# The last two blocks of the last expert become a third pair whose first layer is seven products of halves

## The chip, the cores and the metric

One core of one Trainium2 chip. The time is that of one run of the whole program, in microseconds (us) of device time; lower is better. The program is shown through one profiled execution, whose own time is given beside the median of the timed runs. TensorE is called PE, VectorE DVE, ScalarE ACT, GpSimd POOL and SyncE SP, as in the profile.

## The reference

```python
# attention with decay, then a mixture of 4 experts over 2304 tokens, then 8 slot experts
scores = scale * q @ k.T + decay;  attn = softmax(scores, causal);  x = attn @ v     # x: 2304 x 512
p = domain_probs / domain_probs.sum(-1)
for e in range(4):
    h = np.maximum(x @ w1[e], 0.0)            # w1[e]: 512 x 1024
    out += p[:, e:e + 1] * (h @ w2[e])        # w2[e]: 1024 x 512
logits = out @ phi                            # 32 slots
d = softmax(logits, axis=0);  slot_input = d.T @ out
slot_out[e2] = relu(slot_input[e2] @ w1_2[e2]) @ w2_2[e2]     # 8 experts, 4 slots each
result = softmax(logits, axis=1) @ slot_out
```

## The kernel before, in words

The change lies in the first mixture of experts, in its last expert (e = 3). The 2304 tokens are 18 tiles of 128; three tiles are a block of 384 tokens, and blocks 0 to 5 cover all. Every float32 factor is held as a high and a low half-precision part, and each product is three matmuls (high by high, high by low, low by high).

A block's expert is two layers. The plain first layer (mm_l1, L642) is 8 groups of 12 matmuls, each 128x128 by 128x384 into one PSUM bank; of each group ACT makes the high part of relu (L648) and DVE the low part (L651). The plain second layer (mm_l2, L660) makes 24 matmuls of 128x512 for one tile, and DVE adds the result, weighted, to the tile's sum (L666).

Where two blocks are a pair, the first layer is cheaper. x of the two blocks and w1 are cut into halves, and seven products of halves (each 6 matmuls of 128x384, with sums of halves of x named s1 to s4 made once and kept) give what eight would. One `quad` (L872 to L900) does this for one of four pieces of 128 columns of the first layer's two halves. Its products come in the order m1, m2, m5, m6, m7, m4, m3, in three kinds of PSUM bank, qA, qF and qE. Between them ACT copies a bank into SBUF (L895) and takes relu (L883), and DVE adds a copy into a bank or into SBUF (L879, among these the add called t22 below) and makes low parts (L886). Some products wait for these: m7 accumulates into the qA bank that ACT has to have copied after m6 (the copy c6), and m4 into the qA bank of which t22 was made after m7. A second form, `quad_sums`, also halves the second layer; its products of the second layer are L1081.

Before the change expert 3 has two pairs (blocks 0 to 3), both in the second form, and blocks 4 and 5 are done plainly: for each, 8 groups of L642 and then three tiles of L660.

After expert 3 has finished a block, its "post" work goes on beside the next block: transposes pt (L2325, copied by ACT L2329 and DVE L2327), logits lg (L2335, with a maximum on DVE and exponentials on ACT), a transpose dt (L2353), slot sums sl (L2360), a transpose ct (L2376, with DVE L2379, L2380, ACT L2382, DVE L2383), and then the split of the result (DVE L2388, and L2390 three times) and one DMA that transposes it (L2392), which is issued from ACT's queue. The last block's post is done tile by tile (L2317 for its pt, copied by ACT L2320). In between stand the two small transposes sel (L2238), written into the first bank of a PSUM pool that is opened when the q banks are given up. Then come the slot experts (L2580, L2597), whose 33.5 MB of weights are loaded by SP (`fill`, L2272) as pages of SBUF come free.

Each engine takes its instructions in the order in which the program issues them. For DVE, ACT, POOL and SP that order comes from a planner with a cost for every task (the number in `T("DVE", 0.55, ...)`); PE's order inside a pair is written out (`in_order`), with `beside()` where one piece of post work is slipped in. Behind the pairs all is in the order of the code.

Of the kernel before, what the change touches and what calls it, by code (L numbers as in the profile page):

```python
# [9 lines left out]
F32 = mybir.dt.float32  # L10
# [3 lines left out]
AF = mybir.ActivationFunctionType  # L14
# [10 lines left out]
T_W, CAP_W = 15, 60  # L25
X_SHIFT = 4
C_MUL = 1024.0
PAIRS = (0, 3, 3, 2)
PLAIN = (0, 1, 0, 0)
ORDER = ((), (0, 1, 2), (2, 0, 1), (0, 1))  # L30
OUT_H = ((), (1, 2), (0, 1), (0, 1))
T_SO = 13
BIG = float(2 ** 23)
# [261 lines left out]
def moe_attention_kernel(ctx: ExitStack, tc: tile.TileContext, q, k, v, f, probs, w1, w2, phi, s1, s2, out):  # L295
# [354 lines left out]
    def ev_l1_b(ps, m):  # L650
        nc.vector.scalar_tensor_tensor(out=hl[:, m], in0=ps, scalar=0.0, in1=hh[:, m], op0=ALU.max, op1=ALU.subtract)  # L651

    def mm_l2(e, j, t, ms=range(KF), ps=None):
        if ps is None:
            ps = ps_m.tile([128, DM], F32, tag="m", name="pso")
        ts = slice(t * 128, (t + 1) * 128)
        h_, l_ = hT2[j % 2 if j < 2 * PAIRS[e] else 0]
# [157 lines left out]
    def halves_tasks(e, w1_t, w2_t, s_t, tmps, between=lambda j: [], used_up=None, plain_t=None, next_x=None, t_sums=None):  # L815
# [39 lines left out]
        def quad(p, m, h_t):  # L855
# [23 lines left out]
                return T("DVE", 0.55, -30, lambda: nc.vector.tensor_tensor(out=out(), in0=x(), in1=y(), op=ALU.add), deps)  # L879

            def split(i, c, y, t, give=None):
                h_, l_ = (z[:, y] for z in hT2[i])
                t = T("Act", 0.52, -30, lambda: nc.scalar.activation(out=h_, in_=c(), func=AF.Relu), [t])  # L883

                def lo():
                    nc.vector.scalar_tensor_tensor(out=l_, in0=c(), scalar=0.0, in1=h_, op0=ALU.max, op1=ALU.subtract)  # L886
                    if give:
                        later(lambda: q_used.update({give: q_used[give] - 1}))
                h_t[i][y] = t = T("DVE", 0.62, -30, lo, [t])
                return t  # L890
# [283 lines left out]
        for p in ORDER[e]:  # L1174
# [801 lines left out]
    with tc.manual_schedule():  # L1976
# [117 lines left out]
        def sums_of_x(p, key, tmp, deps):  # L2094
            s_t[p] = steps(key, x_sums(p, lambda: [page(x, 2)[:, 0:2 * NB] for x in tmp]), X_COST, deps)
# [6 lines left out]
        s_d = [[dram.tile([128, 2 * NB], F32, name=f"sd{p}{i}") for i in range(4)] for p in range(NBLK // 2 - 1)]  # L2102

        def s_place(p, i):
            n = len(p_S[p])
# [19 lines left out]

        def keep_s(p):
            return [T("DMA", 1.0, 90, lambda i=i: nc.sync.dma_start(out=s_d[p][i], in_=s_place(p, i)), s_t[p]) for i in range(4)]
        kept_s = {1: keep_s(1)}
        HOME = 0
        for k, p in (((1, 1), 1), ((1, 2), 2), ((2, 2), 2), (None, HOME)):  # L2130
            xR[k] = [xT[2 * p], xT[2 * p + 1], xS[p]]
# [17 lines left out]
        hq_own[1, 2] = {"11": h_of(xT_page[0]), "22": h_of(xT_page[1])}  # L2149
        hq_own[1, 1] = {**hq_own[1, 2], "12": h_of(wA + 4)}  # L2150
        hq_free[1, 1] = {"11": kept_x[0], "22": kept_x[1], "12": s_t[2]}
        hq_free[2, 0] = {"11": kept_x[4], "22": kept_x[5]}
        hq_free[1, 2] = {"12": kept_x[3], "4": kept_x[2]}
        end_s1, end_1, _ = halves_tasks(1, w1_1 + e0_t, w2_1 + pw_t, s_t, tmps, plain_t=(w1_p, e0_t, plain_l1),
# [19 lines left out]
        def next_2(p, t, old):  # L2174
            i = ORDER[2].index(p) + 1
            n = (ORDER[2] + ORDER[3])[i]
            if n in s_t:
                (x_2 if i < 3 else x_3)[n] = load_x(n, [t])
            else:
                back = [T("DMA", 2.0, 30 + x, lambda x=x: nc.sync.dma_start(out=page(xT_page[x], 3), in_=x_d[x]),  # L2180
                          kept_x[x] + [prod[1, 2, i, t] for i in (1, 4) for t in range(TPB)] + raw_end[x]) for x in range(2)]
                sums_of_x(n, 59.8, (n_kn, n_kn + 3), back + [t] + old)
# [23 lines left out]
        kept = {acc_page[T] for T in range(NTILE)} | set(range(hT_p, hT_p + 6)) | set(range(raw2, raw2 + 6)) | {wA + 14, wA + 15} | set(range(p0_, p0_ + 6))  # L2206
# [198 lines left out]
        def used_up(p):  # L2405
            if p == 0:
                dyn.free(p0_, 6)
            if p == PAIRS[e] - 1:
                dyn.free(raw2, 6)
            fill(0)  # L2410

        def next_3(p, t, old):
            x_3[p + 1] = load_x(p + 1, [t], p + 1 < PAIRS[e])
            if p + 1 == PAIRS[e]:
                b12, am = page(wA + 14, 2).rearrange("p (k n) -> p k n", k=2), ams["w1", e]
                y = T("DMA", 1.46, 29, lambda: nc.sync.dma_start(
                    out=b12, in_=w1[e, 0:256, 512:1024].rearrange("(k p) n -> p k n", p=128)), w1_3)
                y = T("Act", 1.14, 62, lambda: nc.scalar.activation(out=wS[e][3][:, 0], in_=b12, func=AF.Copy,
                                                                    scale=am[:, 7:8]), [y, t])
                end_b.append(T("DVE", 1.28, 62, lambda: nc.vector.scalar_tensor_tensor(  # L2420
                    out=wS[e][3][:, 1], in0=b12, scalar=am[:, 7:8], in1=wS[e][3][:, 0], op0=ALU.mult, op1=ALU.subtract),
                    [y], sb=2))
        end_b = []
        end_s3, end_3, rest = halves_tasks(e, [], [], x_3, tmps, between, used_up, next_x=next_3, t_sums=sums_3)
        end_3 = end_3 + end_b
# [4 lines left out]
        for p in t_pages + p_T + [wA + 14]:  # L2430
            dyn.free(p, 2)
        for p in h_pages:
            dyn.free(p, 3)
        for x in range(2):
            xT_page[NBLK - 2 + x], xT[NBLK - 2 + x] = xT_page[x], xT[x]
# [12 lines left out]
        j = NBLK - 1  # L2448
        for mm, ev in moe_quanta(e, j)[:KF]:
            ev(mm())  # L2450
            step(1 + (len(side) > KF))
        while side:
            step(1)
        dyn.free(xT_page[j], 3)
        for p in w_pg:
            dyn.free(p, 2)
        fill(0)
        cells = {}
# [8 lines left out]
        def part(t, ms):  # L2467
            cells[t] = mm_l2(e, j, t, ms, cells.get(t))
            if ms[-1] == KF - 1:
                ev_l2(cells[t], e, j, t)  # L2470

        def second_w(i):

            for p in p_w[0]:
                dyn.free(p + i)
            fill(0)
        po = [post([j * TPB + t], j) for t in range(TPB)]
        (tr0, lg0, dt0, sl0), (tr1, lg1, dt1, sl1), (tr2, lg2, dt2, sl2) = (x[0] for x in po)
# [7 lines left out]
        part(2, (0, 1))  # L2486
        second_w(0)
        rest.pop()()
        tr1()
        sl0()  # L2490
        part(2, (2,))
        rest.append(lg1())
        part(2, (3,))
        second_w(1)
        part(2, (4, 5))
        second_w(2)
        dt1()
# [212 lines left out]
```

## Time and profile before

| | |
|---|---|
| timed runs | 965.05 us median of 3 (964.74 to 966.63) |
| profiled execution, its own time | 965.62 us |
| its span, first to last instruction | 963.9 us |
| mean granted TensorE clock | 0.995 |
| busy PE, DVE, ACT, POOL | 925.5, 696.8, 501.6, 447.8 us |

The span is shorter than the execution's own time by 1.7 us, which lie around the instructions. An engine's busy share is a mean over stages with different limits; a stage's own limit is read from its windows and waits. Ends of matmuls are modelled, so two following matmuls overlap by a little in the rows; the step from one start to the next is the measured one.

### The profile page before, as it was taken

What the parts mean: (1) busy time and instruction counts of PE and PEld (TensorE: products, weight loads), DVE (VectorE), ACT (ScalarE), POOL (GpSimd) and SP (SyncE); (2) the same over time, 40 slices, a digit from 0 to 9 for tenths busy, and PEclk for the clock granted to TensorE, in tenths of its full rate; (3) what the DMA queues carried; (4) which work ended last, traced back from release to release, by engine and by line L of the source; (5) the groups of instructions that cost most, each with busy time, mean ns of one, the idle gap of its engine ahead of it and who ended that gap; (6) DMA issues with size and microseconds to landing.
All of it is one profiled execution on the core that took longest, in us unless ns stands there. A gap on an engine that the chain in (4) does not pass through costs nothing.

```text
span 963.9 us, 22484 instructions
## 1 busy us (share of the span) xinstructions
PE 925.5 (96%) x9092; PEld 637.4 (66%) x9092; DVE 696.8 (72%) x1329; ACT 501.6 (52%) x1115; POOL 447.8 (46%) x440
## 2 busy tenths in 40 slices
PE   6988999999999999999999999999999999999994
PEld 3567778788778775456868645686868768655331
DVE  6989987878786579959779796868976585433313
ACT  5887888877787565446053842525453250212123
POOL 3998786786664368435058323635543150000000
PEclk9999999999999999999999999999999999999998
DMA  8889999999999740341202444231413032954695
GB/s 225 190 158 176 187 189 187 184 205 166 203 163 246 127 165 35 137 142 60 89 1 67 153 153 153 95 114 44 169 65 132 1 97 82 382 175 134 192 361 196
DMA packets 265320, 144.51 MB, mean 150 GB/s; under 512 B 230880, under 2 KB 230880, under 8 KB 265216
## 3 DMA queue, kind: packets, MB, share of 16 engines
q1 hardware_dynamic: 263088, 142.51, 58.2%
q8 instruction: 71, 1.16, 0.5%
q10 hardware_dynamic: 2128, 0.57, 0.3%
q14 instruction: 33, 0.27, 0.1%
HBM read 88.78 MB, written 12.58 MB: 105 GB/s over the span
## 4 chain that ended last, share of the span: by engine, by line
PE 75%; DVE 13%; issue 3%; ACT 2%; POOL 2%; DMA 2%; SPq 1%; DVEq 0%; ACTq 0%; POOLq 0%
PE qA L942 9%; PE qA L1081 7%; PE pso L1144 6%; PE psh L599 6%; PE pso L620 6%; PE qE L942 5%; PE qE L1081 5%; PE psh L642 3%; PE qF L1081 3%; PE pso L660 3%; PE s L1579 3%; PE pso L1081 2%; PE qF L942 2%; PE pv L1668 2%; DVE arena L552 2%
## 5 line engine op out<-in xcount | busy, mean ns | idle before, releaser
L1081 PEld LDWEIGHTS <-arena 128*128 128x128 f16 x1512 | 147.8, 98 | 21.1 <-issue 1.8
L942 PEld LDWEIGHTS <-arena 128*128 128x128 f16 x1008 | 98.4, 98 | 66.5 <-issue 3.8
L1448 POOL TENSOR_SCALAR arena<-arena 128x384 f16<-128x384 f32 (+5 forms) x77 | 56.8, 741 | 136.2 <-ACT arena L953 76.1
L972 POOL TENSOR_TENSOR arena<-arena 128x384 f16<-128x384 f32 x78 | 78.6, 1017 | 75.0 <-ACT arena L1446 73.4
L942 PE MATMUL qA<-arena 128*128 128x384 f16 x576 | 104.5, 326 | 0.7 <-DVE arena L959 0.3
L599 PE MATMUL psh<-arena 128*128 128x128 f16 x1728 | 101.9, 219 | 0.0
L620 PE MATMUL pso<-arena 128*128 128x512 f16 x432 | 100.6, 384 | 0.0
L599 PEld LDWEIGHTS <-arena 128*128 128x128 f16 x1728 | 97.4, 98 | 0.4
L1446 ACT ACTIVATE arena<-arena 128x384 f16<-128x384 f32 (+5 forms) x137 | 79.6, 593 | 29.7 <-DVE arena L964 22.2
L1620 ACT ACTIVATE arena<-s,mx,qs 128x320 f32<-128x320 f32 (+4 forms) x144 | 91.5, 641 | 4.8 <-POOL arena L1637 1.8
L1637 POOL TENSOR_TENSOR arena<-arena 128x128 f16<-128x128 f32 (+4 forms) x79 | 69.5, 901 | 12.9 <-ACT arena L1446 11.1
L704 POOL TENSOR_TENSOR arena<-arena 128x768 f32<-128x768 f32 (+2 forms) x23 | 46.4, 2024 | 54.8 <-DVE arena L704 37.6
L1600 DVE TENSOR_REDUCE mx<-s 128x1 f32<-128x576 f32 (+4 forms) x76 | 64.3, 848 | 8.1 <-PE s L1579 7.8
L620 PEld LDWEIGHTS <-arena 128*128 128x128 f16 x432 | 40.5, 99 | 44.4 <-issue 2.1
L1579 PE MATMUL s<-arena 128*128 128x128 f16 (+1 forms) x928 | 65.1, 212 | 4.3 <-ACT arena L1620 3.4
L1081 PE MATMUL qA<-arena 128*128 128x256 f16 x576 | 68.8, 273 | 0.0
L1144 PE MATMUL pso<-arena 128*128 128x512 f16 x288 | 63.3, 379 | 0.0
L1579 PEld LDWEIGHTS <-arena 128*128 128x128 f16 x928 | 57.5, 98 | 7.1 <-issue 5.2
L552 DVE SCALAR_TENSOR_TENSOR arena<-arena,wm 128x512 f16<-128x512 f32 x44 | 55.3, 1269 | 1.9 <-ACT arena L549 1.9
L1637 DVE TENSOR_TENSOR arena<-arena 128x64 f16<-128x64 f32 (+4 forms) x69 | 49.9, 760 | 6.6 <-POOL arena L1448 3.4
L942 PE MATMUL qE<-arena 128*128 128x384 f16 x288 | 53.7, 326 | 0.1
L953 ACT ACTIVATE arena<-qA 128x384 f32<-128x384 f32 x48 | 23.3, 486 | 57.9 <-PE qA L942 56.8
(277 smaller groups left out, 1872.8 us busy)
## 6 DMA issues: line engine op xcount, KB each, us to landing
arena<-in_moe_w_dram SPq DMA_DIRECT2D x61, 512.0 KB, 4.6
arena<-in_moe_w_dram SPq DMA_DIRECT2D x63, 256.0 KB, 5.1
arena<-xd SPq DMA_DIRECT2D x10, 768.0 KB, 4.3
arena<-in_moe_w_dram SPq DMA_DIRECT2D x7, 1024.0 KB, 9.0
arena<-in_moe_w_dram SPq DMA_DIRECT2D x7, 768.0 KB, 10.6
xd<-arena SPq DMA_DIRECT2D x6, 768.0 KB, 7.1
arena<-sd SPq DMA_DIRECT2D x12, 384.0 KB, 6.1
arena<-in_k_dram SPq DMA_DIRECT2D x16, 256.0 KB, 3.7
```

The source lines that it names most:

```text
L552: return lambda: nc.vector.scalar_tensor_tensor(out=wS[e][o][:, 1, c], in0=b, scalar=am[:, 7:8], in1=wS[e][o][:, 0, c], op0=ALU.mult, op1= ...
L599: nc.tensor.matmul(out=ps[:, m, :], lhsT=wt["w1" + a, 0][:, kk, ms], rhs=xT[j][:, b + kk, ts], start=(n == 0), stop=(n == 3 * KD - 1))
L620: nc.tensor.matmul(out=ops[u], lhsT=a[:, m, ts], rhs=wt["w2" + b, 0][:, m, :], start=(m == 0 and z == 0), stop=(m == KF - 1 and z == 2))
L942: nc.tensor.matmul(out=ps[c], lhsT=wS[e][o][:, w, k, ms], rhs=a[z][:, k], start=(first and i == 0), stop=(i == 5), skip_group_check=True)
L972: h_t[q][m] = y = T(LO, {"DVE": 0.55, "Pool": 1.0}, -30, lambda eng: by[eng].tensor_tensor(out=l_, in0=a, in1=h_, op=ALU.subtract), [y], r ...
L1081: nc.tensor.matmul(out=ps[c, t], lhsT=hq[a][x][:, m, ts], rhs=wq[y][:, m, :], start=(first and m == 0 and n == 0), stop=(m == KF // 2 - 1 ...
L1144: nc.tensor.matmul(out=cell[0], lhsT=a[:, m, ts], rhs=wt["w2" + b, e][:, m, :], start=(len(left) == KF - 1 and z == 0), stop=(not left and ...
L1446: nc.scalar.activation(out=out, in_=x, func=AF.Copy, scale=scale)
L1579: nc.tensor.matmul(out=o, lhsT=qT[u][:, 2 * h + w, :], rhs=kT[kk][:, 2 * h + w, k0:k0 + n_], start=(w == 0), stop=(w == 1 and mask is None))
L1600: nc.vector.tensor_reduce(out=mx[:, 0:nh].rearrange("p (a h) -> p a h", a=sv.shape[1]), in_=sv, axis=AX.X, op=ALU.max, negate=True)
L1620: nc.scalar.activation(out=P[:, x], in_=sv[:, x // hb, x % hb], func=AF.Exp, scale=qs[u][:, 4:5], bias=mxs[n][:, 4 + x:5 + x], accum_out=s ...
L1637: by[eng].tensor_tensor(out=t[:, :, d0:d0 + n_], in0=P[:, :, s0:s0 + n_], in1=t[:, :, s0:s0 + n_], op=ALU.subtract)
```

## The change

Expert 3 gets a third pair, blocks 4 and 5. Its first layer is four `quad`s; then follow the plain second layers of both blocks, block 4's three tiles and block 5's three tiles (`part`). The sums s1 to s4 of these blocks, which were made before expert 1, are saved to DRAM (`keep_s(2)`) and loaded again; this replaces one 512 KB load of a quarter of w1 and the ACT and DVE instruction that split it again (L2416 to L2420). The post of block 2 is slipped between the products of the third pair, that of block 3 between second layers of block 4, and that of block 4 between second layers of block 5. SBUF pages come free in another order.

```diff
-PAIRS = (0, 3, 3, 2)
+PAIRS = (0, 3, 3, 3)
-ORDER = ((), (0, 1, 2), (2, 0, 1), (0, 1))
+ORDER = ((), (0, 1, 2), (2, 0, 1), (0, 1, 2))
...
+    def h_at(e, i):
+        return 1 - i if e == E - 1 else i
...
             def split(i, c, y, t, give=None):
-                h_, l_ = (z[:, y] for z in hT2[i])
+                h_, l_ = (z[:, y] for z in hT2[h_at(e, i)])
...
                 if before:
                     beside()
                 next(g)
+                if e == E - 1:
+                    if m == 1:
+                        in_order(0.0, lambda: used_up(-1), [], lambda: True)
+                    if before:
+                        beside()
                 before = g
+            if e == E - 1:
+                next(before)
+                beside()
+                next(before, None)
+                end_s.append(last[-1])
+                in_order(0.0, lambda p=p: used_up(p), [], lambda: True)
+                end.extend(y for z in h_t for y in z.values())
+                continue
...
-        kept_s = {1: keep_s(1)}
+        kept_s = {1: keep_s(1), 2: keep_s(2)}
...
-        for j in range(2 * PAIRS[e], NBLK - 1):
-            for x, (mm, ev) in enumerate(moe_quanta(e, j)):
-                ev(mm())
-                if x == KF - 1:
-                    dyn.free(xT_page[j], 3)
-                    side.append(fill)
-                step(1 + (len(side) > 11 - x))
-            a, z = post(list(range(j * TPB, (j + 1) * TPB)), j)
-            side += a + z + [fill]
+        cells = {}
+
+        def part(k, ms):
+            j, t = NBLK - 2 + k // TPB, k % TPB
+            cells[k] = mm_l2(e, j, t, ms, cells.get(k))
+            if ms[-1] == KF - 1:
+                ev_l2(cells[k], e, j, t)
...
+        for ms in ((0, 1), (2, 4), (5, 6), (3, 7)):
+            part(0, ms)
+            step(2)
+        for ms in ((0, 1), (2, 3)):
+            part(1, ms)
+            step(2)
+        part(1, (4, 5))
+        step(2)
+        part(1, (6, 7))
...
+        part(2, range(KF))
...
+        a, z = post(list(range((j - 1) * TPB, j * TPB)), j - 1)
+        a = [x for x in a if x] + z
+        for k, ms, n in ((3, (0, 1), 1), (3, (2, 3), 1), (3, (4, 5), 1), (3, (6, 7), 1), (4, (0, 1), 2), (4, (2, 3), 2)):
+            part(k, ms)
+            for _ in range(n):
+                a.pop(0)()
...
-        part(0, range(8))
-        part(1, range(4))
         tr0()
-        part(1, (4, 5))
+        part(4, (4, 5))
         rest = [lg0()]
-        part(1, (6, 7))
+        part(4, (6, 7))
         dt0()
```

Three places where the order of an engine is another. Line numbers of the changed kernel are a few higher: L875 is the matmul of a product, L882 the add, L886 relu, L889 the low part, L898 the copy, L663 the second layer's matmul, L2396 to L2400 the DVE and ACT work behind ct, L2405 and L2407 the split, L2409 the DMA that transposes, L2255 and L2256 sel, L2337 the copy of a tile's pt.

ACT, where the second quad of the third pair begins (qA_11567, qF_11574 and qE_11582 are the banks of the first quad, qA_11632, qF_11641 and qE_11650 those of the second; DMA_TRANSPOSE belongs to the post of block 1). In the change:

```order
L898 ACTIVATE arena_64<-qA_11632 128x384
L886 ACTIVATE arena_64<-qF_11641 128x384
L898 ACTIVATE arena_64<-qE_11650 128x384
L2409 DMA_TRANSPOSE arena_64<-arena_64 128x3x128
L886 ACTIVATE arena_64<-qA_11567 128x384
L898 ACTIVATE arena_64<-qA_11632 128x384
L886 ACTIVATE arena_64<-qE_11582 128x384
```

The same DMA_TRANSPOSE in the kernel before, among the relus of the plain first layer of block 4:

```order
L648 ACTIVATE arena_64<-psh_11608 128x384
L648 ACTIVATE arena_64<-psh_11629 128x384
L2392 DMA_TRANSPOSE arena_64<-arena_64 128x3x128
L648 ACTIVATE arena_64<-psh_11649 128x384
L2329 ACTIVATE arena_64<-pt_11664 128x384
```

Where a relu of the plain first layer stood behind the transposing DMA, there now stand a relu of the first quad and then the second quad's copy c6 (the second row with qA_11632), for which its m7 waits.

DVE at the end of the third pair, in the change (qA_11720 and qE_11737 are banks of the third quad, qA_11812 and qE_11829 of the fourth; ct_11875 is that of the post of block 2):

```order
L882 TENSOR_TENSOR qE_11737<-qE_11737,arena_64 128x384
L889 SCALAR_TENSOR_TENSOR arena_64<-qE_11737,arena_64 128x384
L2396 TENSOR_REDUCE arena_64<-ct_11875 128x3
L2397 TENSOR_TENSOR arena_64<-ct_11875,arena_64 128x96
L2400 TENSOR_REDUCE arena_64<-arena_64 128x3
L882 TENSOR_TENSOR arena_64<-qA_11812,arena_64 128x384
L889 SCALAR_TENSOR_TENSOR arena_64<-arena_64 128x384
L2405 TENSOR_SCALAR arena_64<-arena_64 128x6x32
L2407 SCALAR_TENSOR_TENSOR arena_64<-arena_64 128x2x32 x3
L889 SCALAR_TENSOR_TENSOR arena_64<-qA_11812,arena_64 128x384
L882 TENSOR_TENSOR qE_11829<-qE_11829,arena_64 128x384
L889 SCALAR_TENSOR_TENSOR arena_64<-qE_11829,arena_64 128x384
```

The sixth row is t22 of the fourth quad, now behind three rows of the post of block 2, and the last row, the last use of a q bank, is behind that post's split. On PE m7 of the fourth quad, ct, m4 and m3 follow each other here, then six matmuls L663 and sel.

ACT where the post of block 4 ends, in the change; the DMA_TRANSPOSE is that of block 4, and L2337 is the copy of pt of tile 15, the first tile of block 5:

```order
L2360 ACTIVATE arena_64<-lg_12111,arena_64 96x128
L2363 ACTIVATE arena_64<-arena_64 96x1
L2399 ACTIVATE arena_64<-arena_64 128x96
L2409 DMA_TRANSPOSE arena_64<-arena_64 128x3x128
L2337 ACTIVATE arena_64<-pt_12173 128x4x128
L2360 ACTIVATE arena_64<-lg_12185,arena_64 32x128
```

ACT's order is the same here before and after, but on PE 36 + 6 matmuls L660 stood between this ct and the logits of tile 15 (the pt of that tile among them), and now six do.

## Rows read from the trace of the kernel before

**Rows 1.** The page: busy time of the engines; the chain that ended last.
```profile
PE 925.5 (96%) x9092; PEld 637.4 (66%) x9092; DVE 696.8 (72%) x1329; ACT 501.6 (52%) x1115; POOL 447.8 (46%) x440
...
PE 75%; DVE 13%; issue 3%; ACT 2%; POOL 2%; DMA 2%; SPq 1%; DVEq 0%; ACTq 0%; POOLq 0%
```

**Rows 2.** Windows: length, then busy us and count of PE, PEld, DVE, ACT, POOL.
```profile
785.00:800.00 15.00, 15.00 (x127) 12.13 (x125) 13.66 (x32) 5.52 (x11) 5.53 (x6) 1.00 0.77 268
819.00:900.00 81.00, 81.00 (x521) 44.75 (x519) 31.39 (x94) 15.19 (x43) 0.00 (x0) 1.00 0.66 228
930.00:940.00 10.00, 10.00 (x89) 3.12 (x85) 0.29 (x1) 2.39 (x4) 0.00 (x0) 1.00 0.84 322
948.00:950.00 2.00, 0.38 (x4) 0.14 (x2) 1.51 (x2) 1.55 (x3) 0.00 (x0) 1.00 0.01 3
```

**Rows 3.** Timeline of PE, plain layers, and all L642 (ns min/median/max): start, us, line.
```profile
823.60 4.06 PE L642 MATMUL psh<-arena 128*128 128x384 f16 x24
827.50 1.47 PE L2325 MATMUL pt<-ident,arena 128*128 128x128 f32 x12
...
879.57 7.93 PE L660 MATMUL pso<-arena 128*128 128x512 f16 x36
887.34 0.60 PE L2317 MATMUL pt<-ident,arena 128*128 128x128 f32 x4
887.78 1.46 PE L660 MATMUL pso<-arena 128*128 128x512 f16 x6
...
L642 PE MATMUL psh<-arena x192: 323/326/337, 821.4 to 878.2; 128*128 128x384 f16 x192
```

**Rows 4.** Timeline of PE, end of expert 2's quads; L872's idle over all four.
```profile
558.11 1.14 PE L872 MATMUL qA<-arena 128*128 128x384 f16 x6
559.08 2.75 PE L1144 MATMUL pso<-arena 128*128 128x512 f16 x12
561.67 1.14 PE L872 MATMUL qA<-arena 128*128 128x384 f16 x6
...
  issue: 0.3, 1
```

**Rows 5.** ACT and DVE work of expert 2's quads, by line: ns min/median/max.
```profile
L879 DVE TENSOR_TENSOR arena<-qA,arena x4: 544/546/557, 538.6 to 560.9; 128x384 f32<-128x384 f32 x4
L883 ACT ACTIVATE arena<-qA x4: 490/490/491, 542.3 to 562.8; 128x384 f16<-128x384 f32 x4
L886 DVE SCALAR_TENSOR_TENSOR arena<-qF,arena x4: 545/552/557, 535.3 to 555.9; 128x384 f16<-128x384 f32 x4
L895 ACT ACTIVATE arena<-qA x8: 471/486/491, 532.7 to 557.6; 128x384 f32<-128x384 f32 x8
```

**Rows 6.** The DMA issued from ACT, L2392, and ACT around the one at 842.06.
```profile
L2392 ACTq DMA_TRANSPOSE arena<-arena x5: 1197/1359/1804, 797.7 to 882.2; - x5
...
842.06 1.20 ACTq L2392 DMA_TRANSPOSE arena<-arena  x1
843.31 0.49 ACT L648 ACTIVATE arena<-psh 128x384 f16<-128x384 f32 x1 [2.35 <-issue]
```

**Rows 7.** Timelines of PE, DVE and ACT: posts of blocks 0 and 4, from ct on.
```profile
793.35 0.25 PE L2376 MATMUL ct<-ident,arena 96*128 96x96 f32 x1
793.43 1.47 PE L1081 MATMUL pso<-arena 128*128 128x256 f16 x12
...
793.63 0.26 DVE L2379 TENSOR_REDUCE arena<-ct 128x3 f32<-128x96 f32 x1
...
794.70 0.47 DVE L1092 SCALAR_TENSOR_TENSOR arena<-qA,pw,arena 128x256 f32<-128x256 f32 x1
...
880.27 0.25 DVE L2379 TENSOR_REDUCE arena<-ct 128x3 f32<-128x96 f32 x1
...
881.33 0.34 DVE L2388 TENSOR_SCALAR arena<-arena 128x192 f16<-128x192 f32 x1
...
882.24 1.80 ACTq L2392 DMA_TRANSPOSE arena<-arena  x1
```

**Rows 8.** Timelines of PE and ACT: pt, logits and dt of single tiles.
```profile
888.04 0.60 ACT L2320 ACTIVATE arena<-pt 128x512 f32<-128x512 f32 x1 [6.91 <-PE pt L2317]
...
904.27 0.60 PE L2464 MATMUL warm<-ident_h 128*128 128x512 f16 x2
...
905.38 0.25 PE L2353 MATMUL dt<-ident,arena 32*128 32x32 f32 x1 [0.24 <-ACT arena L2343]
```

More of the change, by code (lines that the diff above doesn't have):

```diff
@@ L656, in mm_l2 @@
         ts = slice(t * 128, (t + 1) * 128)
-        h_, l_ = hT2[j % 2 if j < 2 * PAIRS[e] else 0]
+        h_, l_ = hT2[h_at(e, j % 2)]
         for m in ms:
@@ L2101, in moe_attention_kernel @@
         x_d = [dram.tile([128, 3 * 512], F32, name=f"xd{j}") for j in range(NBLK)]
-        s_d = [[dram.tile([128, 2 * NB], F32, name=f"sd{p}{i}") for i in range(4)] for p in range(NBLK // 2 - 1)]
+        s_d = [[dram.tile([128, 2 * NB], F32, name=f"sd{p}{i}") for i in range(4)] for p in range(NBLK // 2)]
         def s_place(p, i):
@@ L2151, in moe_attention_kernel @@
         hq_free[1, 1] = {"11": kept_x[0], "22": kept_x[1], "12": s_t[2]}
+        hq_own[3, 1] = {"1": hq["4"], "4": hq["1"]}
         hq_free[2, 0] = {"11": kept_x[4], "22": kept_x[5]}
@@ L2181, in next_2 @@
                           kept_x[x] + [prod[1, 2, i, t] for i in (1, 4) for t in range(TPB)] + raw_end[x]) for x in range(2)]
[L2182 removed]
+                sums_of_x(n, 59.8, (n_kn, n_kn + 3), back + [t] + old + kept_s[2])
                 x_2[n] = back + s_t[n]
@@ L2205, in moe_attention_kernel @@
         w_pg = [p_wS[0], p_wS[0] + 2, p_wS[1], p_wS[1] + 2]
-        kept = {acc_page[T] for T in range(NTILE)} | set(range(hT_p, hT_p + 6)) | set(range(raw2, raw2 + 6)) | {wA + 14, wA + 15} | set(range(p0_, p0_ + 6))
+        kept = {acc_page[T] for T in range(NTILE)} | set(range(hT_p, hT_p + 6)) | set(range(raw2, raw2 + 6)) | set(range(p0_, p0_ + 6))
         kept |= {p + i for p in w_pg for i in range(2)} | {p + i for p in p_w[0] for i in range(4)}
@@ L2407, in used_up @@
                 dyn.free(p0_, 6)
+            if p < 0:
+                for x in p_T:
+                    dyn.free(x, 2)
+                for x in range(2, NBLK):
+                    dyn.free(xT_page[x], 3)
+                dyn.free(n_kn + 2)
+                dyn.free(n_kn + 5)
             if p == PAIRS[e] - 1:
@@ L2412, in next_3 @@
         def next_3(p, t, old):
[L2413 to L2423, printed above, removed]
+            if p + 1 < PAIRS[e]:
+                x_3[p + 1] = load_x(p + 1, [t])
         end_s3, end_3, rest = halves_tasks(e, [], [], x_3, tmps, between, used_up, next_x=next_3, t_sums=sums_3)
-        end_3 = end_3 + end_b
         sc.run(lambda: all(x.end is not None for x in end_3))
@@ L2429, in moe_attention_kernel @@
         ps2.append(ctx.enter_context(tc.tile_pool(name="ps2", bufs=5, space=PSUM)))
-        for p in t_pages + p_T + [wA + 14]:
+        for p in t_pages + w_pg + [n_kn, n_kn + 3]:
             dyn.free(p, 2)
-        for p in h_pages:
-            dyn.free(p, 3)
         for x in range(2):
-            xT_page[NBLK - 2 + x], xT[NBLK - 2 + x] = xT_page[x], xT[x]
+            dyn.free(xT_page[2 * HOME + x], 3)
         mg = page(dyn.alloc(1))
@@ L2438, in moe_attention_kernel, with second_w @@
         fill(0)
-        for j in range(2 * PAIRS[e], NBLK - 1):
-            for x, (mm, ev) in enumerate(moe_quanta(e, j)):
-                ev(mm())
-                if x == KF - 1:
-                    dyn.free(xT_page[j], 3)
-                    side.append(fill)
-                step(1 + (len(side) > 11 - x))
-            a, z = post(list(range(j * TPB, (j + 1) * TPB)), j)
-            side += a + z + [fill]
-        j = NBLK - 1
-        for mm, ev in moe_quanta(e, j)[:KF]:
-            ev(mm())
-            step(1 + (len(side) > KF))
+        cells = {}
[4 more added lines that the diff above has]
+                ev_l2(cells[k], e, j, t)
+        def second_w(i):
+            for p in p_w[0]:
+                dyn.free(p + i)
+            fill(0)
+        j = NBLK - 1
+        po = [post([j * TPB + t], j) for t in range(TPB)]
+        for ms in ((0, 1), (2, 4), (5, 6), (3, 7)):
[7 more added lines that the diff above has]
+        part(1, (6, 7))
         while side:
             step(1)
-        dyn.free(xT_page[j], 3)
-        for p in w_pg:
-            dyn.free(p, 2)
+        part(2, range(KF))
+        for p in (wA + 8, wA + 11):
+            dyn.free(p, 3)
         fill(0)
-        cells = {}
+        a, z = post(list(range((j - 1) * TPB, j * TPB)), j - 1)
[4 more added lines that the diff above has]
+                a.pop(0)()
+        fill(0)
+        (tr0, lg0, dt0, sl0), (tr1, lg1, dt1, sl1), (tr2, lg2, dt2, sl2) = (x[0] for x in po)
         wps = bank("warm")
@@ L2465, in warm @@
                                  stop=True)
[L2467 to L2478, printed above, removed]
-        part(0, range(8))
-        part(1, range(4))
         tr0()
-        part(1, (4, 5))
+        part(4, (4, 5))
         rest = [lg0()]
-        part(1, (6, 7))
+        part(4, (6, 7))
         dt0()
-        part(2, (0, 1))
+        part(5, (0, 1))
         second_w(0)
@@ L2490, in moe_attention_kernel @@
         sl0()
-        part(2, (2,))
+        part(5, (2,))
         rest.append(lg1())
-        part(2, (3,))
+        part(5, (3,))
         second_w(1)
-        part(2, (4, 5))
+        part(5, (4, 5))
         second_w(2)
         dt1()
-        part(2, (6,))
+        part(5, (6,))
         rest.pop()()
         sl1()
-        part(2, (7,))
+        part(5, (7,))
         second_w(3)
```

## The prediction

> **What bounds the kernel now.** The page comes first: PE is busy 925.5 us of the 963.9 us span, and three quarters of the chain that ended last is PE [rows 1]. That mean covers many stages, so the next view is the windows around the change. From 785 to 800, in the pair stage, and from 819 to 900, in the plain blocks, PE is busy for the whole of each window, while DVE has 31.39 of 81 us and ACT 15.19 [rows 2]. PE is therefore the limit just where the change takes work from it, and each microsecond less of matmuls counts in full, as long as nothing that DVE or ACT make is late. The slot experts behind are still PE's: 930 to 940 is full too [rows 2].
>
> The timeline then gives PE's prices. A group of 12 plain first-layer matmuls takes 1.95 us (24 of them from 823.60 to 827.50), a second-layer matmul 0.2157 us (36 from 879.57 to 887.34 make 7.77) [rows 3]. A product of six in expert 2's quads, which run the same code, takes 0.97 us (558.11 to 559.08) [rows 4]; I use half a group, 0.975.
>
> **What the change removes from PE.** Blocks 4 and 5 have 192 first-layer matmuls now [rows 3], 16 groups: 16 x 1.95 = 31.2 us. Four quads of seven products are 28 x 0.975 = 27.3 us. Saved: **3.9 us**. The second layers, the posts and the slot experts keep their matmuls. The load of w1 that goes, and its split, were beside a full PE (785 to 800) [rows 2]: they are worth nothing. The four saves of sums in expert 1 and the four loads of them stand in SP's queue long before they are wanted; I price them at nothing, and their bound is 1 us of disturbance.
>
> **What it adds: waits.** Plain layers ask little of ACT and DVE. A quad's later products wait for what these two make of the earlier ones, and both take their work in the program's order, in which the posts stand too. I followed that order with measured durations: add, relu, low part and copy 0.55, 0.49, 0.55 and 0.49 us [rows 5]; the split's rows 0.9 us (881.33 to 882.24) [rows 7]; handovers of 0.2 to 0.3 from PE (793.43 to 793.63, 887.78 to 888.04) [rows 3, 7, 8] and about 0.05 from ACT or DVE. The largest price is that of the transposing DMA. It stands in ACT's queue for 1.20 to 1.80 us, 1.36 in the middle, and ACT does nothing else then: after the one of 842.06 with 1.20 us the next ACT instruction starts at 843.31, with no releaser but "issue" [rows 6]. In the plain stage nothing urgent stood behind it. In the new order there are five places:
>
> S1, m7 of the second quad. From the end of its m2, DVE adds (done at 0.79), ACT takes relu (1.32), DVE makes the low part (1.91), then the split of block 1's post (2.70); then come the DMA (2.74 to 4.10), a relu (4.6) and the copy c6 (5.05); m7 can start at 5.1. PE has four products meanwhile, 3.9. Stall **1.2**; 1.05 to 1.65 over the DMA's range.
>
> S2, dt of block 2's post. It comes one product, 0.975, after the logits. Its exponentials took 1.11 us with their handovers (904.27 to 905.38) [rows 8]: **0.15**.
>
> S3, m4 of the fourth quad. From the end of m7, the third quad's last low part on DVE ends at 0.94, the three rows of ct take until 1.93 (the step from the first of them to the next DVE row was 1.07, 793.63 to 794.70) [rows 7], and the add t22 until 2.48. Cover on PE is one ct of 0.08 (793.35 to 793.43) [rows 7]. In expert 2 twelve second-layer matmuls, 2.59 us (559.08 to 561.67), stood here [rows 4]. Stall **2.45**; 2.0 to 2.6.
>
> S4, sel. It writes into a bank of the pool that is opened over the q banks, so it waits for the last low part of the fourth quad. From the end of t22: relu 0.57, low part 1.17, split 1.9, DMA 3.3, relu of m4's bank 3.75, its low part 4.3, the add of m3 4.8, relu 5.4, low part 6.0, sel at 6.1. PE has two products and six second-layer matmuls, 1.95 + 1.29 + 0.05 = 3.3. Stall **2.8**; 2.6 to 3.3.
>
> S5, logits of tile 15. The post of block 4 now ends with its ct and split right ahead of that tile. From ct: DVE starts at 0.28, the split 1.06 later (880.27 to 881.33) and takes 0.9 [rows 7], so the DMA goes from 2.25 to 3.6, and the copy of pt, 0.60 [rows 8], ends at 4.2. PE has ct, four transposes of 0.44 (887.34 to 887.78) [rows 3] and six second-layer matmuls, 0.08 + 0.44 + 1.29 = 1.8. Before, 36 second-layer matmuls stood between. Stall **2.4**; 2.25 to 2.9.
>
> The sum of S1 to S5 is 9.0 us (8.1 to 10.6), and less 3.9 that makes **+5.1 us**. The profiled execution's span of 963.9 with 1.7 around it is 0.6 above the median, and stalls and savings add to either alike: against the median of 965.05 the forecast is **970.2 us**, with 969.2 to 971.8 from the bounds, and 972.8 with the disturbance in expert 1.
>
> [...]
>
> **Rivals.** (A) The waits don't come: *faster*. Expert 2's four quads had 0.3 us of idle over 168 matmuls [rows 4], with all DVE and ACT work in order too. If the third pair ran so, only the 3.9 would be left, 961.1 us. Against it: there a piece of second layer lay between m7 and m4, and no post work stood in the queues. It decides if the handovers and the post's rows together stay below the cover, which for S3 is 0.08. Chance 0.06.
>
> (B) The transposing DMA does not hold ACT, as the idle behind it at 843.31 [rows 6] could be one of the issue itself: S1 goes, S4 and S5 shrink by 1.36 to 1.45 and 1.05. With S2 and S3 that is 5.1, less 3.9: +1.2, 966.3 us, about even. Against it: in [rows 6] the next ACT row follows the end of the DMA by 0.05. Chance 0.10.
>
> (C) The clock. Stalls of 2.4 to 2.9 us in a PE that had none could cost its granted clock. [...] Chance 0.05.
>
> [...]
>
> (D) Weight pages come free later, or the saves in expert 1 delay its loads. Before, the window of 930 to 940 shows a full PE with the DMA engines at 0.84 [rows 2], so the weights were in time, but by how much no row tells. A wait of 2 us there, beside the stalls, makes 972 to 974. Chance 0.07.
>
> **How the numbers follow.** The forecast's own case has 0.72. A measurement of this kernel tells a change of 0.2%, 1.9 us, from none. Slower by more: forecast, (C) and (D), 0.84. Within: (B), 0.10. Faster: (A), 0.06. The range goes from (B) at 966.3 to 974.0, the end of (D), and leaves out (A), (C) and the outer parts of (B) and (D), under 0.2 together.
>
> **What would show it.** In the changed trace PE has 168 matmuls of products in the third pair in place of 192, in 27.3 us without their idle. Idle of 1 us or more stands ahead of four PE rows: a qA product released by ACT's copy, shortly behind the first transposing DMA of the stage; a qA product released by DVE's add, right behind a ct; sel, released by DVE's low part from qE; and lg of the first single tile, released by ACT's copy of pt. If one of the four runs without idle, that step is wrong; if the DMA in ACT's queue is shorter there than 1.2 us, S1, S4 and S5 are all too large. Idle in the slot experts that was not there before, or a clock below 1.00 ahead of 958, would make the time longer than I say. The forecast fails as a whole if the planner's order of issue lets the posts' rows wait on DVE without anything behind them being wanted.

## The result, and the profile after

The changed kernel takes 973.64 us (median of 6 runs, 972.0 to 974.39), the kernel before 965.1 us (median of 6). The ratio is 1.0086, with a 95% interval of 1.0073 to 1.0099: slower by 8.5 us by the medians and 8.3 by the ratio, where 5.1 were forecast. The time lies in the forecast range of 966.3 to 974.0, near its upper end.

The page of the changed kernel, busy time of the engines and the chain that ended last, against [rows 1]:

```profile
PE 924.1 (95%) x9068; PEld 635.4 (65%) x9068; DVE 702.4 (72%) x1338; ACT 507.6 (52%) x1128; POOL 449.6 (46%) x440
...
PE 73%; DVE 13%; ACT 3%; DMA 3%; issue 3%; POOL 2%; SPq 2%; ACTq 0%; DVEq 0%; POOLq 0%
```

There are 24 matmuls fewer, as the edit says, but PE's share of the chain falls too: the time is in waits. PE's timeline shows where (start, us, engine, line, operation, tiles, count, and in brackets the idle time ahead and what ended it). L875 is a product's matmul and L663 the second layer's:

```profile
434.08 3.08 PE L945 MATMUL qA<-arena 128*128 128x384 f16 x18 [0.46 <-ACT arena L956]
...
446.17 1.14 PE L945 MATMUL qE<-arena 128*128 128x384 f16 x6 [1.18 <-DVE arena L967]
...
820.18 0.25 PE L2393 MATMUL ct<-ident,arena 96*128 96x96 f32 x1
...
832.64 1.14 PE L875 MATMUL qE<-arena 128*128 128x384 f16 x6
834.65 1.14 PE L875 MATMUL qA<-arena 128*128 128x384 f16 x6 [0.88 <-ACT arena L898]
...
843.88 1.15 PE L875 MATMUL qA<-arena 128*128 128x384 f16 x6
845.09 0.30 PE L2370 MATMUL dt<-ident,arena 96*128 96x96 f32 x1
...
853.19 0.25 PE L2393 MATMUL ct<-ident,arena 96*128 96x96 f32 x1
855.67 1.14 PE L875 MATMUL qA<-arena 128*128 128x384 f16 x6 [2.24 <-DVE arena L882]
856.64 1.14 PE L875 MATMUL qE<-arena 128*128 128x384 f16 x6
857.62 1.46 PE L663 MATMUL pso<-arena 128*128 128x512 f16 x6
861.74 0.61 PE L2255 MATMUL sel<-ident,arena 128*128 128x128 f32 x2 [2.67 <-DVE arena L889]
862.15 2.76 PE L663 MATMUL pso<-arena 128*128 128x512 f16 x6
864.71 1.07 PE L2342 MATMUL pt<-ident,arena 128*128 128x128 f32 x6
865.62 1.46 PE L663 MATMUL pso<-arena 128*128 128x512 f16 x6
...
893.60 1.46 PE L663 MATMUL pso<-arena 128*128 128x512 f16 x6
897.28 1.06 PE L2352 MATMUL lg<-arena 128*32 128x128 f32 x8 [2.22 <-ACT arena L2337]
```

The three rows of the kernel before that these are compared with:

```profile
444.72 1.14 PE L942 MATMUL qE<-arena 128*128 128x384 f16 x6
...
818.73 0.25 PE L2376 MATMUL ct<-ident,arena 96*128 96x96 f32 x1
...
889.16 1.06 PE L2335 MATMUL lg<-arena 128*32 128x128 f32 x8
```

All five forecast waits are there, each ahead of the row and ended by the engine that was named (the row of dt has no bracket; the view of its tile names ACT's exponentials). The idle in brackets starts at the modelled end of the matmul ahead; measured from where that work's next start would have been, the waits are 1.03 (834.65 less 832.64 + 0.975), 0.23, 2.40, 2.83 and 2.39 us: 8.9 together, where 9.0 were forecast.

Two things were not in the sum. In expert 1 PE has two idle rows, 1.64 us together, of which the kernel before has none of over 0.3. And six second-layer matmuls behind sel take 2.56 us (862.15 to 864.71), where the next six take 1.30. The windows of this stretch (length, busy us of the engines, then the granted clock, ahead of the last two columns) tell why:

```profile
861.00:862.00 1.00, 0.26 (x2) 0.29 (x3) 0.56 (x1) 0.01 (x1) 0.00 (x0) 0.91 1.09 293
862.00:865.00 3.00, 3.00 (x10) 1.33 (x9) 0.50 (x2) 0.00 (x0) 0.00 (x0) 0.50 1.06 399
```

TensorE's granted clock was 0.50 from 862 to 865, right behind two waits of 2.4 and 2.8 us with 3.2 us of work between them. The sel pair, six matmuls and six transposes were slow: 0.19 + 1.27 + 0.25 = 1.7 us.

From ct to the logits of tile 15 it is 70.43 us in the kernel before (818.73 to 889.16) and 77.10 after (820.18 to 897.28), 6.67 more: -3.9 + 8.9 + 1.7 = 6.7. Behind it the rows keep their distance (tile 16's pt starts at 901.93 before and at 910.04 after, 8.11 later). With 1.45 ahead of it (446.17 against 444.72 for the same product in expert 1: the 1.64, less 0.19 by which this execution was ahead there) that is the 8.1 by which the span grew (972.0 against 963.9).

### The profile page after: what moved, and what is told of

The parts are those of the page before. It is cut to its first block, busy times and chain, and to the rows that moved or that the text cites. A ratio compares the mean times of both kernels' runs of the same rounds, so it can differ in the third digit from the quotient of the medians.

```text
span 972.0 us, 22479 instructions
## 1 busy us (share of the span) xinstructions
PE 924.1 (95%) x9068; PEld 635.4 (65%) x9068; DVE 702.4 (72%) x1338; ACT 507.6 (52%) x1128; POOL 449.6 (46%) x440
## 4 chain that ended last, share of the span: by engine, by line
PE 73%; DVE 13%; ACT 3%; DMA 3%; issue 3%; POOL 2%; SPq 2%; ACTq 0%; DVEq 0%; POOLq 0%
PE qA L945 9%; PE qA L1084 6%; PE pso L620 6%; PE pso L1147 6%; PE psh L599 6%; PE qE L1084 5%; PE qE L945 4%; PE qF L1084 3%; PE pso L663 3%; PE s L1595 3%; PE qA L875 3%; PE pso L1084 2%; PE pv L1684 2%; PE qF L945 2%; DVE arena L552 2%
## 5 line engine op out<-in xcount | busy, mean ns | idle before, releaser
L975 POOL TENSOR_TENSOR arena<-arena 128x384 f16<-128x384 f32 x80 | 80.6, 1018 | 77.6 <-ACT arena L1462 75.8
```

What stands on the lines that cost most here:

```text
L975: h_t[q][m] = y = T(LO, {"DVE": 0.55, "Pool": 1.0}, -30, lambda eng: by[eng].tensor_tensor(out=l_, in0=a, in1=h_, op=ALU.subtract), [y], r ...
```

## The experiments

Each ratio compares a kernel with the kernel before on the same chip. What a variant gains over the changed kernel is a difference between two such comparisons, each with an interval of 1 to 2 us either way, so a gain of 1 or 2 us rests on the rows of its trace; a trace is one execution. A useful length in it is the one from the ct at the start of the third pair to the logits of tile 15, 77.10 us in the changed kernel. In the profiles the line numbers move by a few where code was added. Diffs show the main lines; what is left out is marked.

**The saves alone.** The kernel before with the four saves.

```diff
-        kept_s = {1: keep_s(1)}
+        kept_s = {1: keep_s(1), 2: keep_s(2)}
...
-                sums_of_x(n, 59.8, (n_kn, n_kn + 3), back + [t] + old)
+                sums_of_x(n, 59.8, (n_kn, n_kn + 3), back + [t] + old + kept_s[2])
```

> The kernel before, with the four saves of the kept sums of blocks 4 and 5 in expert 1 added and nothing else of the change. Theory: these saves stand in SP's queue ahead of a weight load of the next expert; its split is late on ACT and DVE, and PE idles there for about 1.5 us in all (1.45 in the changed kernel), so the time is 965.1 + 1.5 = 966.6 us. Rival: the idle in expert 1 of the changed kernel comes from another of its edits; then 965.1 us and no PE idle over 0.3 us between 400 and 450.

Measured: 966.97 us, ratio 1.0017 (1.0008 to 1.0027). Its timelines of PE, SP and ACT in expert 1:

```profile
433.15 3.34 PE L942 MATMUL qA<-arena 128*128 128x384 f16 x18 [0.46 <-ACT arena L953]
445.49 1.14 PE L942 MATMUL qE<-arena 128*128 128x384 f16 x6 [1.18 <-DVE arena L964]
...
418.69 2.99 SPq L2127 DMA_DIRECT2D sd<-arena  x4
...
424.99 0.38 SPq L498 DMA_DIRECT2D arena<-in_moe_w_dram  x1
...
430.81 1.06 ACT L507 ACTIVATE arena<-arena 128x1024 f16<-128x1024 f32 x1 [0.67 <-DMA arena<-in_moe_w_dram]
```

These are the same two idle rows, to the hundredth. ACT waits for a weight load that stands behind the saves, and what follows on ACT and DVE is late. The load is issued no later than before (19.37 us behind the first load of this stretch, at 405.62; 19.36 in the kernel before, 406.76 to 426.12). What is late is its landing: ACT's split of it starts 25.19 us behind that first load, and 23.95 before.

**Cover ahead of m4.** The changed kernel, with a piece of block 4's second layer between the fourth quad's m7 and m4.

```diff
             if e == E - 1:
+                def go(p=p):
+                    m_take("early")
+                    early[0] = mm_l2(e, 2 * p, 0, (0, 1, 4, 5))
+                in_order(2.6, go, w2_t + [h_t[0][m] for m in (0, 1, 4, 5)], m_can)
                 next(before)
...
```

> The changed kernel, with 12 second-layer matmuls of block 4's first tile moved between the fourth quad's m7 and m4, as expert 2 has it. Theory: m4 waits for an add behind post rows on DVE; 2.6 us of cover take away the 2.4 us there, sel still waits 2.7 us. Where the granted clock's fall to 0.50 around 862 to 865 (1.7 us) needs both gaps, it goes too: 973.6 - 2.4 - 1.7 = 969.5 us. Rival on the clock: the gap ahead of sel is enough by itself, 971.2 us with a fall behind sel. Rival on the wait: m4 waits as long as before behind the moved piece, 973.6 us or more.

Measured: 972.73 us, ratio 1.0076 (1.0057 to 1.0095). On PE (L876 is a product):

```profile
854.75 2.75 PE L663 MATMUL pso<-arena 128*128 128x512 f16 x12
857.35 1.14 PE L876 MATMUL qA<-arena 128*128 128x384 f16 x6
...
863.20 0.61 PE L2260 MATMUL sel<-ident,arena 128*128 128x128 f32 x2 [2.45 <-DVE arena L890]
```

The wait of m4 is gone, and up to the logits of tile 15 the trace is 2.62 us shorter (821.67 to 896.15). The median fell by 0.9 us only: the granted clock still falls behind sel (0.83 in 860 to 865 and in 865 to 870), and in this execution a second time behind those logits (0.50 in 898 to 900), where the way to tile 16's pt takes 14.35 us in place of 12.76. One gap was enough here; that both are needed was wrong.

**Sel later.** The changed kernel, with block 4's first tile done whole ahead of sel.

```diff
-        for ms in ((0, 1), (2, 4), (5, 6), (3, 7)):
-            part(0, ms)
-            step(2)
+        part(0, range(KF))
+        for k, ms in ((1, (0, 1)), (1, (2, 3)), (1, (4, 5)), (1, (6, 7)), (2, (0, 1)), (2, (2, 3)), (2, (4, 5))):
+            part(k, ms)
+            step(2)
...
```

> The changed kernel, with sel and the post of block 3 behind it moved back by 24 second-layer matmuls. Theory: sel waits for the last use of a q bank, 6.1 us behind the fourth quad's t22, and PE now has 8 us of work until then: its 2.8 us go, and with one gap of 2.4 us left the clock does not fall, another 1.7 us: 973.6 - 4.5 = 969.1 us. Rival: the gap ahead of m4 alone lowers the clock, 970.8 us. Rival: sel's wait is the opening of the new pool and follows wherever the first tile of it stands, then 973.6 us with the same idle at the new place.

Measured: 970.23 us, ratio 1.0053 (1.0038 to 1.0068).

```profile
854.90 1.17 PE L875 MATMUL qA<-arena 128*128 128x384 f16 x6 [2.24 <-DVE arena L882]
855.87 2.11 PE L875 MATMUL qE<-arena 128*128 128x384 f16 x6
857.77 7.39 PE L663 MATMUL pso<-arena 128*128 128x512 f16 x30
865.00 0.38 PE L2255 MATMUL sel<-ident,arena 128*128 128x128 f32 x2
```

Sel no longer waits. The clock now falls behind the gap ahead of m4 (0.66 in 855 to 860): m3 takes 1.90 us (855.87 to 857.77) for 0.97, and from m4 to sel it is 10.10 us where the same matmuls at full clock take 8.42. The rival on the clock holds, 970.8 forecast.

**The split of block 4's post later.**

```diff
-        for k, ms, n in (... (4, (0, 1), 2), (4, (2, 3), 2)):
+        for k, ms, n in (... (4, (0, 1), 2), (4, (2, 3), 1)):
...
         rest.append(lg1())
+        a.pop(0)()
```

> The changed kernel, with the split of block 4's post and its transposing DMA moved from ahead of tile 15 to behind the logits of tile 16. Theory: the logits of tile 15 wait for ACT's copy, which stands behind that DMA; their 2.4 us go and nothing waits behind the DMA at its new place: 973.6 - 2.4 = 971.2 us. Rival: the wait moves with the DMA to the dt or the copy behind it, 973.6 us with idle ahead of dt of tile 16 or pt of tile 17.

Measured: 970.23 us (968.52 to 972.26), ratio 1.0052 (1.0033 to 1.0072). The logits of tile 15 have no idle ahead, and no other row has it instead. From ct to these logits it is 73.09 us (819.04 to 892.13), 4.01 less: 2.4 of the wait and 1.6 because no fall of the clock costs time here. In this execution the clock fell at the gap ahead of m4 (0.97 in 845 to 855, 0.71 in 855 to 860):

```profile
854.53 2.08 PE L875 MATMUL qA<-arena 128*128 128x384 f16 x6 [2.23 <-DVE arena L882]
...
860.57 0.41 PE L2255 MATMUL sel<-ident,arena 128*128 128x128 f32 x2 [0.99 <-DVE arena L889]
```

From m4's start to sel's it is 6.04 us here and 6.07 in the changed kernel, where the clock was 1.00 up to 861: the slow products fill PE's wait for sel, which DVE and ACT set. The fall there cost nothing where sel waited anyway; it cost 1.7 us in the run before, where sel did not wait. The one behind sel cost 1.7 in the changed kernel, the one behind the logits 1.6 in the run with the cover.

**The transposing DMA from SP's queue.**

```diff
-                nc.scalar.dma_start_transpose(out=cT[:, T0:T0 + N, :], in_=c16[:, w].rearrange("p t a s -> p (t a s)"))
+                nc.sync.dma_start_transpose(out=cT[:, T0:T0 + N, :], in_=c16[:, w].rearrange("p t a s -> p (t a s)"))
```

> The changed kernel, with the transposing DMA of each post issued from SP's queue instead of ACT's; all else in its place. Theory: the DMA holds ACT for its whole 1.2 to 1.8 us. Without it the wait of the second quad's m7 goes (1.0 us), the logits of tile 15 wait for nothing (2.4 us), and sel waits 0.9 us in place of 2.8; m4 of the fourth quad still waits its 2.4 us, since only DVE rows stand ahead of it. 973.6 - 1.0 - 2.4 - 1.9 = 968.3 us while one fall of the granted clock (1.7 us) follows the gap ahead of m4, 966.6 us without one. Rival: the DMA does not hold ACT, and the waits come from the rows of DVE; 973.6 us with the four waits where they were.

Measured: 967.67 us, ratio 1.0027 (1.0014 to 1.004). First ACT of the changed kernel, at the second quad, then of this one, the same two instructions (relu of the first quad's qA, and c6):

```profile
832.49 1.20 ACTq L2409 DMA_TRANSPOSE arena<-arena  x1
833.73 0.49 ACT L886 ACTIVATE arena<-qA 128x384 f16<-128x384 f32 x1 [2.27 <-PE qA L875]
834.12 0.48 ACT L898 ACTIVATE arena<-qA 128x384 f32<-128x384 f32 x1
```

```profile
832.97 0.49 ACT L886 ACTIVATE arena<-qA 128x384 f16<-128x384 f32 x1 [0.41 <-PE qA L875]
834.01 0.49 ACT L898 ACTIVATE arena<-qA 128x384 f32<-128x384 f32 x1 [0.54 <-PE qA L875]
```

In the first, the relu starts 0.04 us behind the end of the DMA's row; PE, which its bracket names, did not hold it: in the second, each starts when PE is done with its bank, the relu 1.87 us earlier by the distance from ct (11.68 for 13.55). The waits of m7 and of the logits are gone, sel's too (the clock fell behind m4, 0.66 in 855 to 860, and made PE late there), and m4's stays at 2.24. The DMA's hold on ACT is thus most of three of the five waits.

**All three moves.** The edits of the cover and of the split as above, and the first tile's rest ahead of sel:

```diff
-        for ms in ((0, 1), (2, 4), (5, 6), (3, 7)):
-            part(0, ms)
-            step(2)
+        part(0, (2, 6))
+        part(0, (3, 7))
...
```

> The changed kernel with all three moves: 12 second-layer matmuls ahead of m4, sel behind the rest of the first tile, the split of block 4's post behind the logits of tile 16. Theory: the three large waits and with them every fall of the clock go; left are the wait of m7 in the second quad (1.0 us), that of dt (0.2) and the 1.6 us in expert 1: 965.1 - 3.9 + 1.0 + 0.2 + 1.6 = 964.0 us, granted clock 1.00 from 815 to the end of the second layers. Rival: each wait taken away shows another one behind it (a posts' row late, a PSUM bank not free), 967 us or more.

Measured: 966.15 us, ratio 1.0012 (1.0002 to 1.0021). The three waits are gone and the clock stays at 1.00, but one new wait shows, on PE and behind the same DMA on ACT (L887 is relu):

```profile
861.22 2.28 PE L663 MATMUL pso<-arena 128*128 128x512 f16 x9 [1.11 <-ACT arena L887]
...
857.84 1.20 ACTq L2414 DMA_TRANSPOSE arena<-arena  x1
859.08 0.49 ACT L887 ACTIVATE arena<-qA 128x384 f16<-128x384 f32 x1 [2.73 <-PE qE L876]
860.67 0.49 ACT L887 ACTIVATE arena<-qE 128x384 f16<-128x384 f32 x1 [1.10 <-DVE qE L883]
```

With the whole first tile ahead of sel, PE reaches the last columns of the hidden layer before ACT has made their relu. This wait is 1.3 of the 2.1 us by which the time exceeds the 964.0 forecast; the rest stays open. In the next run, with the DMA on SP, it is gone.

**The moves, the DMAs on SP, and the saves later.**

```diff
-        kept_s = {1: keep_s(1), 2: keep_s(2)}
+        kept_s = {1: keep_s(1)}
...
         w1_2, last = prep_tasks(2, 0, R + [p0_, p0_ + 2], last, [end_s1[-1]], 60)
+        kept_s[2] = keep_s(2, w2_2)
...
```

> The three moves, the transposing DMAs issued from SP, and the saves of the sums of blocks 4 and 5 made to wait until the weights of expert 2's second layer are split, so that they stand behind its loads in SP's queue. Theory: nothing is left of the waits but dt's 0.2 us; the fewer matmuls count in full: 965.1 - 3.9 + 0.2 = 961.4 us, faster than both kernels. Rival: the saves disturb another load in expert 2, or the slot experts' weights come late: 963 us or more.

Measured: 961.38 us, ratio 0.996 (0.9947 to 0.9973): faster than both kernels, with the matmuls saved and no idle of 0.2 us left ahead of a PE row in this stretch. From ct to the logits of tile 15 it is 66.90 us (818.10 to 885.00), 3.53 less than in the kernel before. The window from 815 to 896 (busy PE first, granted clock ahead of the last two columns):

```profile
815.00:896.00 81.00, 80.94 (x528) 45.29 (x526) 40.07 (x109) 20.75 (x55) 0.00 (x0) 1.00 0.66 236
```

**Useless matmuls in the gaps.** Nothing of the computation is left out; 32 matmuls are added.

```diff
+    def busy(n):
+        ps = ps_m.tile([128, DM], F32, tag="m", name="busy")
+        for _ in range(n):
+            nc.tensor.matmul(out=ps, lhsT=ident_h, rhs=ident_h.unsqueeze(1).to_broadcast([128, 4, 128]), start=True, stop=True)
...
```

> The changed kernel with 32 matmuls whose result nothing reads: 10 ahead of the fourth quad's m4, 12 ahead of sel, 10 ahead of the logits of tile 15, so that PE works through most of each gap; nothing else is moved and no wait is shorter. Theory: the waits stay, but the granted clock does not fall behind them: 973.6 - 1.7 = 971.9 us, no slice of 5 us below 1.00 from 850 to 905. Rival: the slow matmuls behind sel have another cause than idling ahead of them (the weights' transfers, say), 973.6 us or more, with the clock or the matmuls behind sel as slow as before.

Measured: 971.7 us, ratio 1.0075 (1.0056 to 1.0094). PE's timeline, and the window of all three gaps:

```profile
819.71 0.25 PE L2402 MATMUL ct<-ident,arena 96*128 96x96 f32 x1
...
858.43 2.75 PE L821 MATMUL busy<-ident_h 128*128 128x512 f16 x12
861.26 0.41 PE L2264 MATMUL sel<-ident,arena 128*128 128x128 f32 x2
...
895.13 1.06 PE L2361 MATMUL lg<-arena 128*32 128x128 f32 x8
...
850.00:905.00 55.00, 54.79 (x322) 27.12 (x320) 22.58 (x69) 8.96 (x27) 0.00 (x0) 1.00 0.63 229
```

The waits are as long as they were: sel starts 2.83 us behind the end of the six matmuls ahead of it, as before. From ct to the logits of tile 15 it is 75.42 us, 1.68 less, with the clock at 1.00 from 850 to 905: with PE's idling filled, this trace has no slow matmuls, and their time comes back. The medians differ by 1.9, the ratios by 1.1, within their intervals. One of the four executions took 975.1 us at a mean granted clock of 0.990 (the others 971.5 to 971.8 at 0.994 and 0.995); what slowed it is not known.

**Ct later.** The changed kernel, without the `beside()` behind the fourth quad's m7, so that ct follows m4.

```diff
-                    if before:
+                    if before and m < KF // 2 - 1:
                         beside()
                 before = g
```

> The changed kernel with the ct of block 2's post moved from ahead of the fourth quad's m4 to behind it, and the split of that post behind sel; no matmul is moved into the gap. Theory: of the 2.4 us ahead of m4, the three rows of ct on DVE make 1.0, and the add chain without cover 1.4; sel's wait goes from 2.8 to about 1.6, since three rows of ct but no split and no transposing DMA stand ahead of it. Idle rows of 1.3 and 1.4 us there, 965.1 - 3.9 + 1.6 + 1.0 + 0.2 + 1.4 + 1.6 + 2.4 = 969.4 us without a fall of the clock, 971.1 us with one. Rival: the wait ahead of m4 is the missing cover alone and stays at 2.2 in the rows, 971 us or more.

Measured: 971.2 us (969.34 to 973.89), ratio 1.0068 (1.0047 to 1.0089).

```profile
854.95 1.14 PE L875 MATMUL qA<-arena 128*128 128x384 f16 x6 [1.26 <-DVE arena L882]
...
859.77 0.41 PE L2255 MATMUL sel<-ident,arena 128*128 128x128 f32 x2 [1.33 <-DVE arena L889]
```

Both idle rows are those forecast, 1.3 and 1.4: of m4's wait one microsecond is the three rows of the post on DVE, the rest the chain without cover. The profiled execution has no fall of the clock in this stretch (1.00 in every window from 845 to 910) and a span of 968.4, 970.1 us with what lies around it; the runs spread over more than one fall would make, and what they add stays open.

**The saves later, alone.** Only the edit of the saves shown above, on the changed kernel.

> The changed kernel with only the saves of the sums of blocks 4 and 5 moved behind the loads of expert 2's weights in SP's queue. Theory: PE's two idle rows in expert 1 (0.46 and 1.18 us) go and nothing else changes: 973.6 - 1.6 = 972.0 us. Rival: the planner orders DVE and ACT in another way all the same, and idle of over 0.3 us stays between 400 and 455: 973 us or more.

Measured: 972.02 us, ratio 1.0076 (1.0059 to 1.0092). No idle over 0.3 us is left between 400 and 455. The gain in time is within the intervals, and in this trace the clock falls at m4's gap (0.94 in 845 to 855, 0.77 in 855 to 860) and behind the logits (0.83 in 890 to 900); that the two idle rows go with the edit is what the run shows.

## Why the prediction was right, and where it was short

**The saving.** 3.9 us were forecast, and where the waits are taken away the runs agree within their noise: the ratio of 0.996 gives 3.9 us (2.6 to 5.1), the medians on that chip 3.2 (964.58 less 961.38), and the stretch from ct to the logits of tile 15 is 3.53 shorter with dt's 0.2 of wait still forecast in it.

**S1 to S5.** Forecast 1.2, 0.15, 2.45, 2.8 and 2.4; measured 1.03, 0.23, 2.40, 2.83 and 2.39. The causes hold as well: the DMA in ACT's queue for S1, S5 and most of S4 (gone or smaller from SP's queue), the post's rows and the missing cover for S3 (1.0 and 1.4), the last use of a q bank for S4. S1 is a little less, since the DMA took 1.20 us there and not 1.36. In S4 and S5 it was shorter too (1.22 and 1.20); there rows or handovers that the sums had 0.1 to 0.15 too short made it up. S1 and S4 count the split with some 0.8 us where S5 takes the 0.9 of its rows. The row of S1 shows 0.88 us of idle and not the 1 us named as a sign; by the starts it is 1.03.

**"I price them at nothing".** The step that failed is that of the saves in expert 1. They cost 1.6 us, beyond the bound of 1. The four saves were early enough for their own reader; but a weight load stands behind them in the same queue, and it landed late for its own (ACT's split of it 1.24 us later, 25.19 against 23.95, with the saves alone). My sum named the queue and not what is behind it; only rival (D) did, with 0.07.

**Rival (C), the clock.** It came, with a chance of 0.05, and the sum had no term for it. The window of 948 to 950 [rows 2], where 1.62 us of idle left the clock at 1.00, spoke against a fall. But the waits forecast were longer than that one, so it bore on none of them, and it was one execution: in six of the twelve profiles the clock falls behind this same gap. The trace of the kernel before even has a fall that the prediction does not use, in its first tenth, behind a gap of 1.86 us with others of 1.57 and 1.41 in the ten microseconds ahead:

```profile
77.26 0.60 PE L456 MATMUL mp<-ident,kvs 128*128 128x128 f32 x2 [1.86 <-DVE qs L436]
...
78.00:80.00 2.00, 2.00 (x6) 0.76 (x5) 1.90 (x8) 1.77 (x5) 1.58 (x2) 0.50 0.94 214
```

The runs give the price of a fall: 1.7 us behind sel, 1.6 behind the logits, and nothing for the one ahead of sel whose slow matmuls lay in the shadow of the next wait (6.04 us from m4 to sel, against 6.07). With the two terms as measured the sum is -3.9 + 8.9 + 1.6 + 1.7 = +8.3, against 8.5 by the medians (973.64 less 965.1).

**What was luck.** That 973.64 lies in the range is luck in part. The upper end of 974.0 stood for a wait of 2 us in the slot experts, which did not come; the saves and a fall filled the place, 3.3 us together, and the range had left (C) out.

**The other rivals.** (A) needs the waits gone, and they came; only the kernel built without them is at 961.4. (B) falls with ACT's rows in the run on SP's queue. Of (D) only the loads in expert 1 came; the slot experts are shifted as a whole by 8.1 us, with no new idle.

## What to carry to other kernels

A cheaper way to multiply is worth its matmuls only if the engines that finish its pieces keep up: follow each piece's chain through the other engines' queues as issued, with everything that stands in them, and keep independent matmuls for the places where the chain is longer than what PE has. A transposing DMA issued from ACT's queue was an instruction of ACT with a duration of 1.2 us or more; put it on a queue that nobody waits for. Before you price a fall of the clock, look for falls in the whole trace, not at one row. And when a transfer is moved or added, ask whose load comes behind it.

## What the runs showed of the hardware

A gap in PE's work cost more than itself here, 1.7 us more behind sel in the changed kernel. In the seven profiles that have such gaps there were 12 of 2.2 to 2.7 us by the rows; behind 8 of them, in the gap or within about a microsecond of its end, the granted clock went from 1.00 to 0.50, and it stayed there for some 3 us (862 to 865 in the changed kernel, with 0.91 and 0.89 in the microseconds on either side). The same gap in the same place did it in one execution and not in another (2.24 ahead of m4: not in the changed kernel, but in four of its variants). A shorter gap did it too. Behind the 1.62 us near the end of the program, which all twelve profiles have, the clock fell in six of them, in the gap or within about half a microsecond of its end. One of them is the fastest kernel, in its last PE work:

```profile
945.80 5.33 PE L2690 MATMUL out<-arena 128*128 128x512 f16 x15 [1.62 <-DVE arena L2671]
...
946.00:948.00 2.00, 2.00 (x6) 0.70 (x5) 1.48 (x2) 0.99 (x2) 0.00 (x0) 0.50 0.94 360
```

That place has gaps of 0.95 and 0.34 us shortly ahead, and the fall there cost 0.2 us or less: from that gap's end to the last instruction it is 14.1 us here and 13.9 in the kernel before, where the clock stayed at 1.00 through the same PE work. Behind the gaps of 0.7 to 1.4 us between 395 and 940 us no profile shows a fall (the clock was 1.00 from 845 to 865 around the two of 1.26 and 1.33 in the run with ct later), and from 100 to 395 those of the kernel before and of the changed kernel show none. Which gap brings a fall and which does not, these runs show only by such counts.

The transposing DMA of this small tile takes 1.2 to 2.1 us in ACT's queue in the changed kernel, and 1.2 to 2.9 in SP's, where the median plain load of a mixture weight (L498) takes 0.37: by the medians (1.20 and 1.18) it held its issuing queue three times as long.
